# Block attention with soft mixture of experts: loads without pacing, three buffers for values, and stores of 64 rows by two

## The chip, the cores and the metric

The kernel runs on one core of a Trainium2 chip. The metric is device time in microseconds (us) of one execution; before the change it is 456.55 us, the median of three runs (453.82 to 457.1). Inputs and the output lie in the chip's memory, and every transfer between it and the core's on-chip memory is a DMA, issued here by SyncE (SP in the profile) and carried out by 16 DMA engines that belong to the core.

## What is computed

Attention inside chunks of 64 tokens (8 batches, 8 heads, 576 tokens, head size 64), then a mixture of experts in which 32 slots (8 experts with 4 each) are softmax mixtures of all 4608 tokens, and each token takes back a softmax mixture of the slots' outputs. All arrays are float32.

```python
scores = scale * np.matmul(q_c, k_c.transpose(0, 1, 2, 4, 3))      # in each chunk of 64
attn = np.exp(scores - np.max(scores, axis=-1, keepdims=True))
attn = attn / (np.sum(attn, axis=-1, keepdims=True) + 1e-09)
x = np.matmul(attn, v_c)                  # then reshaped to 4608 tokens x 512
logits = x @ phi                          # 4608 x 32
d = softmax of logits over the tokens; slot_input = d.T @ x
h = np.maximum(slot_input[e] @ w1[e], 0.0); slot_out[e] = h @ w2[e]
c = softmax of logits over the slots; out = c @ slot_out
```

q, k and v are 9.44 MB each, w1 and w2 together 33.6 MB, the output is 9.44 MB (4608 rows of 2 KB).

## The kernel before

**Units.** The attention runs over 18 units. A unit is four heads of one batch with 512 of its 576 tokens; the eight chunks of 64 tokens that are left (one of each batch) are gathered into a ninth "batch" that stands in the middle of the list. `load_qk(n)` loads a unit's keys and queries, 512 KB each, into one of two buffers (`kn`, `qn`); `load_v(n)` its values, four DMAs of 128 KB, into one of two buffers `vb`. For the ninth batch the same amounts come in more and smaller DMAs: eight of 128 KB, and eight of 64 KB with 64 partitions each.

**Turns.** `turn(n, order)` writes out one turn by hand; each engine's program is fixed in this order. In turn n TensorE (PE) makes the scores of unit n (`psc`), transposes the probabilities of unit n-1 (`pt`), transposes keys and queries of unit n+2 (`pk`, `pq`), multiplies probabilities and values of unit n-1 (`pav`) and transposes the outputs of unit n-2 (`px`). Every second turn adds the logits of a finished batch (`pl`, `pe`) or its share of the slot inputs (`pp`). VectorE (DVE) takes maxima, subtracts, normalises and copies; ScalarE (ACT) does the exponentials and the other copies. Beside each turn stand DMA issues: the keys and queries of unit n+3 ahead of it, about one of 14 weight tiles `wa` of 1 MB each (two DMAs), and the values of unit n+1 behind it.

**Pacing.** All loads of this stretch go through `dma` (line 87). It keeps a list of the loads issued and makes each new one wait until so many of the earlier ones have landed that no more than MEGA = 2^18 elements (1 MiB) are in flight. Besides, the framework gives each DMA one of eight semaphores in turn, and each engine issues its own instructions in order, so a DMA that waits holds all DMAs behind it.

**Experts.** When attention is through, its buffers become 7 more weight tiles (`wb`). The slot inputs `siT` (line 424) feed the `up` matmuls (line 544); each `up` frees four tiles, into which later weights are loaded without pacing; the `down` matmuls (line 579) accumulate all experts, `spread` copies the result, and `combine(b)` makes 512 output rows: four matmuls, four copies into a free weight tile (lines 613 and 615), four stores. In the store buffer, partition p = 64 sq + x and column block j = 2 i + kh hold row x of chunk 4 i + 2 sq + kh. Before the change, store j takes all 128 partitions of one column block, and they go to chunks c and c + 2:

```python
            c = 4 * (j // 2) + j % 2
            nc.sync.dma_start(rows[c:c + 3:2], ov[:, j])
```

Of the kernel before, what the change touches and what calls it, by code (L numbers as in the profile page):

```python
# [8 lines left out]
F32 = mybir.dt.float32  # L9
# [6 lines left out]
def kernel(  # L16
# [10 lines left out]
    nc = tc.nc  # L27
# [3 lines left out]
    B, H, S, D = q.shape  # L31
    P = 128
    CH = 64
    H2 = P // 2
    NC = S // CH
    UC = 8
    HG = H // 2
# [5 lines left out]
    REST = B  # L43
    vs = list(range(B // 2)) + [REST] + list(range(B // 2, B))
    NL = len(vs)
    NU = 2 * NL
    E, _, FF = w1.shape
    SL = phi.shape[1]
# [2 lines left out]
    EPS = 1e-9  # L51
    NWA = 14
    NWB = 7
    NV = 2
    NQK = 2
    MEGA = 2 ** 18

    HALF = (slice(0, H2), slice(H2, P))
    QUARTERS = ((0, 0), (1, 1), (0, 1), (1, 0))
# [6 lines left out]
    phi_sb = const.tile([P, NF, SL], F32, name="phi_sb")  # L66
# [10 lines left out]
    wa = [wpa.tile([P, 2048], F32, name=f"wa{i}") for i in range(NWA)]  # L77
# [3 lines left out]
    wt = {}  # L81
    worder = [(m, e, h) for m in (1, 2) for e in range(E) for h in range(2)]


    paced = []

    def dma(dst, src, pace=True):
        d = nc.sync.dma_start(dst, src).ins  # L88
        if pace:
            size = 1  # L90
            for m in dst.shape:
                size *= m
            for o in paced:
                o[1] += size
            over = [o[0] for o in paced if o[1] > MEGA]
            if over:
                tc.add_manual_dep(
                    d, over[-1].name,
                    mybir.DependencyInfo(mybir.DependencyClass.Sync, mybir.DependencyReason.DATA),
                    reason="pace")  # L100
            paced.append([d, size])

    def load_w(n, t, pace=True):
        m, e, h = worder[n]
        src = (w1[e].rearrange("(p j) f -> p (j f)", p=P)[:, 2 * FF * h:2 * FF * (h + 1)] if m == 1 else
               w2[e, DM * h:DM * (h + 1)].rearrange("(p g) f -> p (g f)", p=P))
        for i in range(2):
            dma(t[:, 1024 * i:1024 * (i + 1)], src[:, 1024 * i:1024 * (i + 1)], pace)
        t = t.rearrange("p (j f) -> p j f", j=2) if m == 1 else t.rearrange("p (g f) -> p g f", g=4)
        wt[m, e, h] = t  # L110

    with ExitStack() as actx:
        aq = actx.enter_context(tc.tile_pool(name="attn_q", bufs=1))
        a1 = actx.enter_context(tc.tile_pool(name="attn1", bufs=1))
        a2 = actx.enter_context(tc.tile_pool(name="attn2", bufs=2))
# [11 lines left out]
        at = a1.tile([P, 2, 2, HG, CH], F32, name="at")  # L127
        vb = [a1.tile([P, HG, 2, 2, D + 1], F32, name=f"vb{i}") for i in range(NV)]
        xT = [a1.tile([P, 2, 4, P], F32, name=f"xT{i}") for i in range(2)]
# [11 lines left out]
        def unit(n):  # L141
            return vs[n // 2], HG * (n % 2)

        def chunk(b, c):
            return (c, UC * CH) if b == REST else (b, CH * c)

        def load_qk(n, heads=None):
            b, h0 = unit(n)
            for src, dst in ((k, kn[n % NQK]), (q, qn[n % NQK])):
                for hs in heads or [slice(0, HG)]:  # L150
                    if b == REST:
                        for h in range(hs.start, hs.stop):
                            dma(
                                dst[:, h].rearrange("p j d -> p (j d)"),
                                src[:, h0 + h, UC * CH:S].rearrange("b (p j) d -> b p (j d)", j=4),
                            )
                    else:
                        dma(
                            dst[:, hs].rearrange("p h j d -> p h (j d)"),
                            src[b, h0 + hs.start:h0 + hs.stop, 0:UC * CH].rearrange(  # L160
                                "h (p j) d -> p h (j d)", j=4),
                        )

        def load_v(n):

            b, h0 = unit(n)
            for i in range(2):
                for sq in range(2):
                    for kh in range(2 if b == REST else 1):
                        bb, s0 = chunk(b, 4 * i + 2 * sq + kh)  # L170
                        rs, ns = (HALF[kh], CH) if b == REST else (slice(0, P), P)
                        dma(vb[n % NV][rs, :, i, sq, 0:D],
                            v[bb, h0:h0 + HG, s0:s0 + ns].rearrange("h x d -> x h d"))

        psum = {}

# [79 lines left out]
        def values(n, i):  # L256
            psum["v", i] = pp = pair(f"pav_{n}_{i}")
            for h in range(HG):
                for kh, sq in QUARTERS:
                    rs = HALF[kh]  # L260
                    nc.tensor.matmul(  # L261
                        pp[HALF[sq], kh, (D + 1) * h:(D + 1) * (h + 1)],
                        lhsT=at[rs, sq, i, h, :], rhs=vb[n % NV][rs, h, i, sq, :],
                        start=True, stop=True,
# [83 lines left out]
                    nc.tensor.transpose(out=pe[:, r, o:o + H2], in_=src[rs, :], identity=ident[rs, rs])  # L348

        def copy_e(b):  # L350
            eN = a2.tile([P, 4, SL], F32, tag="eN", name=f"eN_{b}")
            nc.scalar.copy(eN.rearrange("p (r j) s -> p r (j s)", r=2), psum["e"][:, :, 0:H2])
            lst[b][0] = eN

# [64 lines left out]
        def slots(wsel, ws):  # L419
# [17 lines left out]
        }  # L437
        batch = {
            "lg": logits, "lT": copy_l, "rm": slot_max, "eT": weights, "pe": turn_e, "eN": copy_e,
            "ca": token_max, "su": sums, "pp": partial, "pr": add_partial, "cx": token_exp, "cc": token_norm,  # L440
        }
# [7 lines left out]
        def turn(n, names):  # L449
            for x in names:  # L450
                if x in batch:
                    b = n // 2 - 2
                    if 0 <= b < NL and n % 2 == (x in odd):
                        batch[x](b)
                elif 0 <= n - lag.get(x, 0) < NU:
                    steps[x](n - lag.get(x, 0))
# [7 lines left out]
        for t in vb:  # L464
            nc.gpsimd.memset(t[..., D:D + 1], 1.0)
        load_v(0)
        nc.vector.reduce_sum(sel, ident.rearrange("p (j s) -> p s j", s=SL), axis=AX.X)
        nc.vector.tensor_copy(rep, sel.unsqueeze(1).to_broadcast([P, 4, SL]))
        nc.vector.memset(one, 1.0)
        warm(12)  # L470
        turn(-2, ["Tk", "kb", "Tq", "q"])
        load_qk(2)
        load_v(1)
        dma(phi_sb, phi.rearrange("(f p) s -> p f s", p=P))
        nw = 0
        for n in range(NU):
            if 0 < n < NU - 3:
                load_qk(n + 3)
            while nw < min(NWA, (NWA * (n + 1) + NU - 1) // NU):
                load_w(nw, wa[nw])  # L480
                nw += 1
            if n == 0:
                turn(0, ["S", "max"])
                turn(-1, ["Tk", "kb", "Tq", "q"])
                load_qk(3)
                turn(0, order[order.index("at"):])
            else:
                turn(n, order)
                if n + 1 < NU:
                    load_v(n + 1)  # L490

        b = NL - 1
        fill = wa[0][:, 0:512]
# [29 lines left out]
    def bank(name):  # L523
        return ps2.tile([P, 512], F32, tag="ps", name=name)

    wb = [wpb.tile([P, 2048], F32, name=f"wb{i}") for i in range(NWB)]
    for t in wb:
        load_w(nw, t, False)
        nw += 1
    free = []  # L530

# [5 lines left out]
    def up(e0):  # L537

        nonlocal nw
        ph = bank(f"ph_{e0}")  # L540
        for j in range(4):
            for i in range(4):
                e, h = e0 + i // 2, i % 2
                nc.tensor.matmul(  # L544
                    ph[SL * i:SL * (i + 1), :],
                    lhsT=siT[:, j, :],
                    rhs=wt[1, e, j // 2][:, j % 2, DM * h:DM * (h + 1)],
                    start=(j == 0), stop=(j == 3),
                )
        hr = f2.tile([P, 512], F32, tag="hr", name=f"hr_{e0}")  # L550
        nc.scalar.activation(hr, ph, AF.Relu, scale=rden)
        for i in range(2 * e0, 2 * e0 + 4):
            t = (wa + wb)[i]
            if nw < len(worder):
                load_w(nw, t, False)
                nw += 1
            else:
                free.append(t)
        return hr
# [45 lines left out]
    def combine(b, ss, ob):  # L605
        ov = ob.rearrange("p (j f) -> p j f", j=4)
        cT = c_all[:, 4 * b:4 * b + 4, :].rearrange("p j s -> p (j s)")
        for j in range(4):
            rs = slice(SL * j, SL * (j + 1))
            pf = bank(f"pf_{b}_{j}")  # L610
            nc.tensor.matmul(pf, lhsT=cT[rs, :], rhs=ss[rs, :], start=True, stop=True)
            if j % 2 == 0:
                nc.scalar.copy(ov[:, j], pf)
            else:
                nc.vector.tensor_copy(ov[:, j], pf)  # L615

        for j in range(4):
            if vs[b] == REST:
                rows = out.rearrange("(s x) f -> s x f", x=S)[:, UC * CH:S]
            else:  # L620
                rows = out[S * vs[b]:S * vs[b] + UC * CH].rearrange("(s x) f -> s x f", x=CH)
            c = 4 * (j // 2) + j % 2
            nc.sync.dma_start(rows[c:c + 3:2], ov[:, j])

    hrs = {}
    for e in range(0, E, 2):
# [12 lines left out]
    for b in range(NL):  # L639
        combine(b, ss, obs[b])  # L640
# [30 lines left out]
```

## Time and profile before

| | |
|---|---|
| median of three runs | 456.55 us |
| profiled execution | 455.94 us, of which the span in the trace is 454.2 us |
| PE, DVE, ACT busy | 218.3 us (48%), 135.9 us (30%), 128.1 us (28%) |
| bytes read and written | 61.93 MB, 9.44 MB |
| first and last score matmuls of a unit | 10.10 us, 200.12 us |
| slot inputs copied | 222.90 us |
| first store issued | 265.80 us |

Times in rows are microseconds from the start of the span. "Busy" is the union of an engine's instructions. The DMA share is the mean busy share of the core's 16 DMA engines. A wait names the engine and line that waited, and what ended the wait.

### The profile page before, as it was taken

To read this page: it belongs to the slowest core of one execution; us is meant where nothing else is said; L and a number is where in the kernel's file an instruction comes from. 1 tells how busy PE (TensorE), PEld (TensorE's weight loads), DVE (VectorE), ACT (ScalarE), POOL (GpSimd) and SP (SyncE) were. 2 spreads that over 40 slices of the span, in tenths; PEclk is the share of its full clock that TensorE was granted. 3 is DMA by queue.
4 is the path that set the end of the run, shared out by engine and by line. 5 is a ranking of instruction groups with operands and counts; after the bars stand their busy time and mean duration, and the time that the engine had idled before them with its cause. 6 is when DMAs were issued, how large, how long until landed. Compare 5 with 4: busy or idle time off the path is not lost.

```text
span 454.2 us, 8764 instructions
## 1 busy us (share of the span) xinstructions
PE 218.3 (48%) x3820; PEld 156.7 (35%) x3820; DVE 135.9 (30%) x281; ACT 128.1 (28%) x210; POOL 6.5 (1%) x25
## 2 busy tenths in 40 slices
PE   6659778677778675998999982000000000000000
PEld 6658666556566564875434140000000000000000
DVE  4227547564456464697300073000000000000000
ACT  4439546553446453664211062000000000000000
POOL 0000000000000000000110000000000000000000
PEclk9669889996889898899899997555555555555555
DMA  6778776775577877879999701111111111111111
GB/s 200 202 229 237 214 229 190 198 217 178 149 219 225 223 225 195 234 234 339 354 306 410 299 19 52 51 51 51 51 51 51 51 51 51 51 51 51 52 51 45
DMA packets 71710, 71.94 MB, mean 158 GB/s; under 512 B 40440, under 2 KB 58872, under 8 KB 71672
## 3 DMA queue, kind: packets, MB, share of 16 engines
q1 hardware_dynamic: 71672, 71.38, 50.2%
q8 instruction: 30, 0.49, 0.4%
q14 instruction: 8, 0.07, 0.0%
HBM read 61.93 MB, written 9.44 MB: 157 GB/s over the span
## 4 chain that ended last, share of the span: by engine, by line
DMA 37%; PE 12%; DVE 5%; SPq 4%; issue 2%; ACT 1%; DVEq 0%; ACTq 0%
DMA wa<-in_moe_w_dram 12%; DMA qn<-in_q_dram 10%; DMA kn<-in_k_dram 8%; DMA vb<-in_v_dram 7%; SPq L88 4%; PE px L285 2%; PE pq L207 2%; PE pav L261 1%; PE ph L544 1%; PE pp L379 1%; DVE xT L293 1%; DVE xs L273 1%; PE psc L224 1%; PE pd L139 1%; DVE wa L615 1%
## 5 line engine op out<-in xcount | busy, mean ns | idle before, releaser
L193 ACT COPY kb<-pk 64x512 f32<-64x512 f32 x72 | 44.9, 623 | 8.7 <-PE pk L184 8.1
L224 PE MATMUL psc<-kb,qT 128*64 128x128 f32 x576 | 38.0, 287 | 5.2 <-ACT qT L211 2.2
L207 PE MATMUL pq<-ident,qn 64*64 64x64 f32 (+1 forms) x576 | 27.6, 261 | 19.0 <-DMA qn<-in_q_dram 18.6
L211 ACT COPY qT<-pq 128x1024 f32<-128x1024 f32 x18 | 18.2, 1013 | 65.6 <-PE pq L207 65.5
L224 PEld LDWEIGHTS psc<-kb,qT 128*64 128x64 f32 x576 | 33.1, 143 | 7.8 <-DVE xT L293 2.9
L207 PEld LDWEIGHTS pq<-ident,qn 64*64 64x64 f32 (+1 forms) x576 | 24.4, 153 | 26.5 <-issue 23.5
L293 DVE COPY xT<-px 128x1024 f32<-128x1024 f32 x16 | 19.6, 1223 | 44.2 <-PE px L285 44.2
L234 DVE TENSOR_REDUCE mx<-psc 128x16 f32<-128x1024 f32 x18 | 22.0, 1221 | 18.6 <-PE psc L224 18.5
L184 PE MATMUL pk<-ident,kn 64*128 64x64 f32 x288 | 15.0, 248 | 23.3 <-DMA kn<-in_k_dram 21.3
L261 PE MATMUL pav<-vb,at 64*64 64x65 f32 x1152 | 24.5, 237 | 1.9 <-DVE xT L293 1.9
L273 DVE TENSOR_TENSOR xs<-pav,rc 128x512 f32<-128x512 f32 x36 | 24.9, 692 | 1.2
L285 PE MATMUL px<-ident,xs 128*128 128x128 f32 x144 | 24.3, 320 | 0.9 <-DVE xs L273 0.8
L261 PEld LDWEIGHTS pav<-vb,at 64*64 64x64 f32 x1152 | 21.2, 148 | 5.2 <-DVE xT L293 2.6
L237 DVE TENSOR_TENSOR sc<-psc,mx 128x1024 f32<-128x1024 f32 x18 | 21.9, 1219 | 0.4
L184 PEld LDWEIGHTS pk<-ident,kn 64*128 64x128 f32 x288 | 12.4, 156 | 26.5 <-issue 22.8
L254 ACT COPY at<-pt 128x1024 f32<-128x1024 f32 x18 | 18.2, 1013 | 9.9 <-PE pt L251 9.9
L285 PEld LDWEIGHTS px<-ident,xs 128*128 128x128 f32 x144 | 19.1, 164 | 4.8 <-issue 2.7
L243 ACT ACTIVATE sc<-sc 128x1024 f32<-128x1024 f32 x18 | 19.0, 1055 | 2.1 <-DVE sc L237 2.1
L544 PE MATMUL ph<-wa,siT 128*32 128x512 f32 x112 | 15.7, 647 | 0.0
L579 PE MATMUL po<-wa,hz 128*32 128x512 f32 x88 | 13.2, 595 | 1.1 <-DMA wa<-in_moe_w_dram 1.0
L251 PE MATMUL pt<-ident,sc 64*128 64x64 f32 x288 | 12.8, 229 | 1.0 <-ACT sc L243 1.0
L251 PEld LDWEIGHTS pt<-ident,sc 64*128 64x128 f32 x288 | 10.4, 139 | 4.2 <-issue 3.1
(87 smaller groups left out, 195.0 us busy)
## 6 DMA issues: line engine op xcount, KB each, us to landing
wa<-in_moe_w_dram SPq DMA_DIRECT2D x50, 512.0 KB
vb<-in_v_dram SPq DMA_DIRECT2D x64, 128.0 KB
kn<-in_k_dram SPq DMA_DIRECT2D x15, 512.0 KB
qn<-in_q_dram SPq DMA_DIRECT2D x15, 512.0 KB
wb<-in_moe_w_dram SPq DMA_DIRECT2D x14, 512.0 KB
out_dram<-wb SPq DMA_DIRECT2D x24, 256.0 KB
out_dram<-wa SPq DMA_DIRECT2D x12, 256.0 KB
kn<-in_k_dram SPq DMA_DIRECT2D x8, 128.0 KB
```

The costliest lines, as they stand in the source:

```text
L184: nc.tensor.transpose(out=pt[:, i, o:o + H2], in_=src[rs, h, 2 * j:2 * j + 2, :].rearrange("p j d -> p (j d)"), identity=ident[rs, rs])
L193: nc.scalar.copy(kbs[n % 2][HALF[a]].rearrange("x i hp c a (p j u) -> x a u (i hp) c p j", j=2, u=2)[:, a, u], pv[HALF[u], a].rearrange("x ...
L207: nc.tensor.transpose(out=pt[0:D * (1 + a), i, o:o + H2], in_=src[rs, f - D * a:f + D], identity=ident[rs, rs])
L224: nc.tensor.matmul(pp[HALF[sq], i, 256 * hp:256 * (hp + 1)].rearrange("p (a k x) -> p a k x", a=2, k=2)[:, :, kh], lhsT=qT[:, i, hp, CH * ...
L234: nc.vector.reduce_max(mx, psum["s"].rearrange("p i (r x) -> p (i r) x", x=CH), axis=AX.X)
L237: nc.vector.tensor_tensor(sc.rearrange("p i h (kh x) -> p (i h kh) x", x=CH), psum["s"].rearrange("p i (r x) -> p (i r) x", x=CH), psum["m ...
L251: nc.tensor.transpose(out=pt[:, sq, o:o + CH], in_=sc[rs, i, h, :], identity=ident[rs, rs])
L261: nc.tensor.matmul(pp[HALF[sq], kh, (D + 1) * h:(D + 1) * (h + 1)], lhsT=at[rs, sq, i, h, :], rhs=vb[n % NV][rs, h, i, sq, :], start=True, ...
L273: nc.vector.tensor_tensor(xs[b % 2][:, 2 * i:2 * i + 2, HG * D * g:HG * D * (g + 1)].rearrange("p k (h d) -> p k h d", d=D), av[..., 0:D], ...
L285: nc.tensor.transpose(out=psum["x"][:, hp, P * j:P * (j + 1)], in_=xs[b % 2][:, j, f:f + P], identity=ident)
L293: nc.vector.tensor_copy(d, r)
L544: nc.tensor.matmul(ph[SL * i:SL * (i + 1), :], lhsT=siT[:, j, :], rhs=wt[1, e, j // 2][:, j % 2, DM * h:DM * (h + 1)], start=(j == 0), sto ...
```

## The change

The list that paces the loads goes; a load now waits for its buffer and for its semaphore's last DMA alone. Values get a third buffer. A unit's loads stand behind each turn in the order keys and queries (of unit n+4), weights, values (of unit n+2). The tile `eN` has one buffer in place of two. A store now takes one half of the partitions and two column blocks, which are two neighbouring chunks of 64 rows.

```diff
-    NV = 2
+    NV = 3
     NQK = 2
-    MEGA = 2 ** 18
 
...
-
-    paced = []
-
-    def dma(dst, src, pace=True):
-        d = nc.sync.dma_start(dst, src).ins
-        if pace:
-            size = 1
-            for m in dst.shape:
-                size *= m
-            for o in paced:
-                o[1] += size
-            over = [o[0] for o in paced if o[1] > MEGA]
-            if over:
-                tc.add_manual_dep(
-                    d, over[-1].name,
-                    mybir.DependencyInfo(mybir.DependencyClass.Sync, mybir.DependencyReason.DATA),
-                    reason="pace")
-            paced.append([d, size])
-
-    def load_w(n, t, pace=True):
+    def load_w(n, t):
         m, e, h = worder[n]
         src = (w1[e].rearrange("(p j) f -> p (j f)", p=P)[:, 2 * FF * h:2 * FF * (h + 1)] if m == 1 else
                w2[e, DM * h:DM * (h + 1)].rearrange("(p g) f -> p (g f)", p=P))
         for i in range(2):
-            dma(t[:, 1024 * i:1024 * (i + 1)], src[:, 1024 * i:1024 * (i + 1)], pace)
+            nc.sync.dma_start(t[:, 1024 * i:1024 * (i + 1)], src[:, 1024 * i:1024 * (i + 1)])
...
-                        dma(vb[n % NV][rs, :, i, sq, 0:D],
-                            v[bb, h0:h0 + HG, s0:s0 + ns].rearrange("h x d -> x h d"))
+                        nc.sync.dma_start(
+                            vb[n % NV][rs, :, i, sq, 0:D],
+                            v[bb, h0:h0 + HG, s0:s0 + ns].rearrange("h x d -> x h d"),
+                        )
 
...
-            eN = a2.tile([P, 4, SL], F32, tag="eN", name=f"eN_{b}")
+            eN = a2.tile([P, 4, SL], F32, tag="eN", name=f"eN_{b}", bufs=1)
...
         for n in range(NU):
-            if 0 < n < NU - 3:
-                load_qk(n + 3)
-            while nw < min(NWA, (NWA * (n + 1) + NU - 1) // NU):
-                load_w(nw, wa[nw])
-                nw += 1
             if n == 0:
                 turn(0, ["S", "max"])
                 turn(-1, ["Tk", "kb", "Tq", "q"])
                 load_qk(3)
                 turn(0, order[order.index("at"):])
+                load_qk(4)
             else:
                 turn(n, order)
-                if n + 1 < NU:
-                    load_v(n + 1)
+                if n + 4 < NU:
+                    load_qk(n + 4)
+            while nw < min(NWA, (NWA * (n + 1) + NU - 1) // NU):
+                load_w(nw, wa[nw])
+                nw += 1
+            if n + 2 < NU:
+                load_v(n + 2)
 
...
-        for j in range(4):
-            if vs[b] == REST:
-                rows = out.rearrange("(s x) f -> s x f", x=S)[:, UC * CH:S]
-            else:
-                rows = out[S * vs[b]:S * vs[b] + UC * CH].rearrange("(s x) f -> s x f", x=CH)
-            c = 4 * (j // 2) + j % 2
-            nc.sync.dma_start(rows[c:c + 3:2], ov[:, j])
+        if vs[b] == REST:
+            rows = out.rearrange("(s x) f -> s x f", x=S)[:, UC * CH:S]
+        else:
+            rows = out[S * vs[b]:S * vs[b] + UC * CH].rearrange("(s x) f -> s x f", x=CH)
+        for i in range(2):
+            for sq in range(2):
+                c = 4 * i + 2 * sq
+                nc.sync.dma_start(rows[c:c + 2].rearrange("k x f -> x k f"), ov[HALF[sq], 2 * i:2 * i + 2])
 
```

The other lines of the diff put `nc.sync.dma_start` in place of `dma`, and drop an argument.

On SP, which issues every DMA, the loads of the third and fourth turn stand as follows (kn and qn are the buffers of keys and queries, vb those of values, wa weight tiles; the numbers tell buffers apart). Before:

```order
L88 DMA wa_80<-in_moe_w_dram 128x1024 x2
L88 DMA vb_115<-in_v_dram 128x4x64 x4
L88 DMA kn_108<-in_k_dram 128x4x256
L88 DMA qn_106<-in_q_dram 128x4x256
L88 DMA wa_81<-in_moe_w_dram 128x1024 x2
L88 DMA vb_116<-in_v_dram 128x4x64 x4
L88 DMA kn_107<-in_k_dram 128x4x256
L88 DMA qn_105<-in_q_dram 128x4x256
```

After, with what each waits for (DMAHW0 to 7 are the eight DMA semaphores, PE the matmuls that read the buffer last):

```order
L138 DMA qn_106<-in_q_dram 128x4x256 [waits DMAHW4_49,PE_49]
L88 DMA wa_80<-in_moe_w_dram 128x1024 [waits DMAHW5_49]
L88 DMA wa_80<-in_moe_w_dram 128x1024 [waits DMAHW6_49]
L152 DMA vb_115<-in_v_dram 128x4x64 [waits DMAHW7_49,PE_49]
L152 DMA vb_115<-in_v_dram 128x4x64 [waits DMAHW0_49]
L152 DMA vb_115<-in_v_dram 128x4x64 [waits DMAHW1_49,PE_49]
L152 DMA vb_115<-in_v_dram 128x4x64 [waits DMAHW2_49]
L138 DMA kn_107<-in_k_dram 128x4x256 [waits DMAHW3_49,PE_49]
L138 DMA qn_105<-in_q_dram 128x4x256 [waits DMAHW4_49,PE_49]
L88 DMA wa_81<-in_moe_w_dram 128x1024 [waits DMAHW5_49]
```

The values moved behind the weights and are those of a later unit, and each load waits for the DMA eight places ahead of it in place of those that the pacing names.

At the end of SP's program stand the stores (out_dram, from the tiles that combine fills). Before:

```order
L88 DMA wa_89<-in_moe_w_dram 128x1024 x2
L623 DMA out_dram<-wa_90 2x64x512 x4
L623 DMA out_dram<-wa_91 2x64x512 x4
L623 DMA out_dram<-wa_92 2x64x512 x4
L623 DMA out_dram<-wb_3424 2x64x512 x4
L623 DMA out_dram<-wb_3425 2x64x512 x4
```

After:

```order
L88 DMA wa_89<-in_moe_w_dram 128x1024 x2
L607 DMA out_dram<-wa_90 64x2x512 x4
L607 DMA out_dram<-wa_91 64x2x512 x4
L607 DMA out_dram<-wa_92 64x2x512 x4
L607 DMA out_dram<-wb_3426 64x2x512 x4
L607 DMA out_dram<-wb_3427 64x2x512 x4
```

Their number and place are the same; the outermost size on the memory's side is 64 in place of 2.

## Rows read from the trace of the kernel before

**Rows 1.** The page: its first line, the slices of the span (40 equal ones; digits are tenths), and the bytes moved.

```profile
span 454.2 us, 8764 instructions
...
PE   6659778677778675998999982000000000000000
...
DMA  6778776775577877879999701111111111111111
GB/s 200 202 229 237 214 229 190 198 217 178 149 219 225 223 225 195 234 234 339 354 306 410 299 19 52 51 51 51 51 51 51 51 51 51 51 51 51 52 51 45
...
HBM read 61.93 MB, written 9.44 MB: 157 GB/s over the span
```

**Rows 2.** The view of stretches: from and to, length, busy time and count of PE, PE's weight loads, DVE, ACT and POOL, the granted clock of PE as a share of full speed, the DMA share, GB/s.

```profile
10.00:200.00 190.00, 142.50 (x3060) 119.33 (x3060) 101.49 (x195) 99.61 (x158) 2.40 (x6) 0.87 0.76 211
...
120.00:123.00 3.00, 3.00 (x56) 2.06 (x56) 1.98 (x3) 1.11 (x2) 0.00 (x0) 0.88 0.39 85
...
184.00:200.00 16.00, 15.18 (x396) 12.74 (x396) 13.92 (x29) 11.22 (x19) 0.40 (x1) 0.95 0.83 229
...
242.00:256.00 14.00, 13.78 (x120) 4.15 (x118) 0.29 (x2) 1.15 (x3) 0.00 (x0) 1.00 1.03 408
...
275.00:435.00 160.00, 0.00 (x0) 0.00 (x0) 1.08 (x2) 0.49 (x1) 0.00 (x0) 0.51 0.13 51
```

**Rows 3.** The timeline from 222 to 300 us, single rows of ACT, PE, SP and DVE: start, length, engine, line, operation, what it writes and reads, count, and in brackets the idle time before it. DVE's last copies into the store buffers run from 268.83 for 7.26 us, to 276.1.

```profile
222.90 0.27 ACT L424 COPY siT<-pst 128x128 f32<-128x128 f32 x1 [3.81 <-PE pst L423]
...
260.26 1.05 PE L579 MATMUL po<-wa,hz 128*32 128x512 f32 x4 [0.21 <-DMA wa<-in_moe_w_dram]
...
265.80 35.67 SPq L623 DMA_DIRECT2D out_dram<-wa  x9
...
268.83 7.26 DVE L615 COPY wb<-pf 128x512 f32<-128x512 f32 x12
```

**Rows 4.** The waits of SP's queue and of PE over the whole span: who waited for what, us in total, times, the longest.

```profile
SPq L88 <- DMA wa<-in_moe_w_dram: 39.2, 37, 2.2
SPq L88 <- DMA vb<-in_v_dram: 30.5, 15, 3.8
SPq L88 <- DMA qn<-in_q_dram: 29.6, 16, 3.1
SPq L88 <- DMA kn<-in_k_dram: 28.5, 18, 3.5
...
PE pk L184 <- DMA kn<-in_k_dram: 21.3, 14, 3.2
PE pq L207 <- DMA qn<-in_q_dram: 18.6, 15, 2.3
```

**Rows 5.** The chain of waits that ended last, a piece of it in order of time: start, length, what; a DMA's length is from issue to landing.

```profile
24.25 4.62 DMA kn<-in_k_dram
28.91 4.52 DMA kn<-in_k_dram
33.45 4.04 DMA wa<-in_moe_w_dram
...
39.07 3.61 DMA vb<-in_v_dram
42.70 4.72 DMA qn<-in_q_dram
```

**Rows 6.** The timeline of PE from 185 to 201 us, two turns and the start of a third; columns as in rows 3.

```profile
185.78 1.97 PE L224 MATMUL psc<-kb,qT 128*64 128x128 f32 x32
187.67 0.71 PE L251 MATMUL pt<-ident,sc 64*128 64x64 f32 x16
188.22 0.68 PE L184 MATMUL pk<-ident,kn 64*128 64x64 f32 x16
...
189.83 1.16 PE L207 MATMUL pq<-ident,qn 64*128 64x64 f32 x32
...
193.33 1.97 PE L224 MATMUL psc<-kb,qT 128*64 128x128 f32 x32 [0.22 <-DVE xT L293]
...
198.44 0.28 PE L348 MATMUL pe<-ident,eT 64*128 64x64 f32 x2 [0.46 <-ACT eT L328]
...
200.12 1.09 PE L224 MATMUL psc<-kb,qT 128*64 128x128 f32 x16 [0.25 <-DVE xT L293]
```

**Rows 7.** The timeline of PE from 8 to 12 us: the first unit's score matmuls.

```profile
10.10 2.20 PE L224 MATMUL psc<-kb,qT 128*64 128x128 f32 x30 [2.16 <-ACT qT L211]
```

**Rows 8.** The timeline of SP: issues of loads, with the time that issuing them took, waits among them included. The eight at 117.69 are values of the ninth batch, 64 partitions each.

```profile
28.91 0.37 SPq L88 DMA_DIRECT2D kn<-in_k_dram  x1
...
16.89 2.04 SPq L88 DMA_DIRECT2D vb<-in_v_dram  x4
...
117.69 6.14 SPq L88 DMA_DIRECT2D vb<-in_v_dram  x8
```

**Rows 9.** SP's issue of the first weights behind attention, and the view of stretches (columns as in rows 2) while those weights are loaded and the experts are computed.

```profile
204.61 12.55 SPq L88 DMA_DIRECT2D wb<-in_moe_w_dram  x14
...
205.00:217.00 12.00, 10.13 (x237) 6.94 (x226) 8.49 (x25) 5.42 (x10) 0.40 (x1) 1.00 1.00 345
220.00:240.00 20.00, 19.65 (x146) 7.90 (x149) 3.42 (x17) 2.85 (x6) 2.89 (x10) 0.91 0.90 326
240.00:260.00 20.00, 19.12 (x149) 6.03 (x141) 0.58 (x4) 2.03 (x4) 0.00 (x0) 1.00 0.92 369
```

More of the change, by code (lines that the diff above doesn't have):

```diff
@@ L152, in load_qk @@
                         for h in range(hs.start, hs.stop):
-                            dma(
+                            nc.sync.dma_start(
                                 dst[:, h].rearrange("p j d -> p (j d)"),
@@ L157, in load_qk @@
                     else:
-                        dma(
+                        nc.sync.dma_start(
                             dst[:, hs].rearrange("p h j d -> p h (j d)"),
@@ L171, in load_v @@
                         rs, ns = (HALF[kh], CH) if b == REST else (slice(0, P), P)
-                        dma(vb[n % NV][rs, :, i, sq, 0:D],
-                            v[bb, h0:h0 + HG, s0:s0 + ns].rearrange("h x d -> x h d"))
+                        nc.sync.dma_start(
+                            vb[n % NV][rs, :, i, sq, 0:D],
+                            v[bb, h0:h0 + HG, s0:s0 + ns].rearrange("h x d -> x h d"),
+                        )
         psum = {}
@@ L473 @@
         load_v(1)
-        dma(phi_sb, phi.rearrange("(f p) s -> p f s", p=P))
+        nc.sync.dma_start(phi_sb, phi.rearrange("(f p) s -> p f s", p=P))
         nw = 0
         for n in range(NU):
-            if 0 < n < NU - 3:
-                load_qk(n + 3)
-            while nw < min(NWA, (NWA * (n + 1) + NU - 1) // NU):
-                load_w(nw, wa[nw])
-                nw += 1
             if n == 0:
@@ L527 @@
     for t in wb:
-        load_w(nw, t, False)
+        load_w(nw, t)
         nw += 1
@@ L554, in up @@
             if nw < len(worder):
-                load_w(nw, t, False)
+                load_w(nw, t)
                 nw += 1
```

## The prediction

> **What bounds the kernel now.** I read the slices of the span first. The three compute engines are busy for the first 60% of it, and then for 40% nothing but DMA works, at one tenth of the DMA engines and some 51 GB/s [rows 1]. So two stretches decide, and I took them apart with the view of stretches. In the last one (275 to 435 us) the DMA share is 0.13 at 51 GB/s, with PE at 0.00 busy; in the weights' stretch (242 to 256 us) the same DMA engines give 408 GB/s at a share of 1.03 [rows 2]. 0.13 is 2 of 16 engines, and 51 is an eighth of 408: the stores run on two engines, each at full speed. The last copies into the store buffers are done at 276.1 us [rows 3], so the span's last 178 us wait for nothing but stores. The arithmetic closes: 9.44 MB written [rows 1] at 51 GB/s are 185 us, after the first store at 265.80 [rows 3] that makes 450.8 of a span of 454.2.
>
> In the first stretch (10 to 200 us) PE is busy 142.5 of 190 us, DVE 101.5, ACT 99.6, and the DMA share is 0.76 at 211 GB/s [rows 2]: no resource is full. The waits say why. SP, which issues every load, waits 127.8 us in total for earlier loads to land (39.2 + 30.5 + 29.6 + 28.5) [rows 4]; these are mostly the pacing waits. PE waits 39.9 us for keys and queries (21.3 + 18.6) [rows 4]. The chain of waits from 20 to 47 us is loads one behind another, each 3.6 to 4.7 us from issue to landing [rows 5]: 1 MiB in flight over some 4.5 us of latency is 233 GB/s, close to the 211 measured.
>
> **The change part by part.**
>
> *Loads in the attention stretch.* Without the pacing list a load waits for its buffer (a PE semaphore) and for the DMA eight places ahead in SP's program, as the order with waits shows; eight loads are one unit's keys, queries, weights and values, 2.5 MiB in place of 1. So the queue should stay filled, and the next limit is PE's turn. One turn that had its loads in time ran from 185.78 to 193.33, 7.55 us, with PE without a gap; the next, from 193.33 to 200.12, took 6.79 without the two transposes of k and q (0.68 and 1.16) and with 0.22 and 0.46 us of waits on DVE and ACT [rows 6], so 8.6 at most with them. Mean: 8.1 us, over 17 turns 137.7 us, in place of the 190.0 from the first score matmul at 10.10 [rows 7] to the last turn's at 200.12. **Gain 52.3 us.** Two bounds: taking PE's 39.9 us of waits out of 190.0 and nothing else leaves 150.1 (gain 39.9); 17 turns of 7.55 leave 128.4 (gain 61.7). I take the middle value, because granted clock in the stretch was 0.87 and was 0.95 where PE ran almost without gaps [rows 2], so waits that go also make the work shorter. DMA could limit as well: a share of 0.76 over 190 us is 144 us of full work, 6.7 more than I take, but at the 408 GB/s of the weights' stretch the same 40.1 MB need only 98 us, so part of the 0.76 is packets that start on an idle queue.
>
> *The new order of a unit's loads* (weights ahead of values, values two units ahead in a third buffer) costs nothing by itself: v of unit n+2 is issued at the end of turn n and first read in turn n+3, two turns (16 us) later, against the 3.6 us of a v load [rows 5]. k and q of unit n+4 are issued when turn n has transposed unit n+2, and needed two turns later. What SP pays is the issue: 0.37 us for a large load, some 2.0 us for four of v [rows 8], in all about 3.5 us of a turn of 8; for the two units of leftover rows 8 small loads take 6.14 us with their waits [rows 8], still inside a turn. If the cover goes there, one or two turns grow by 2 to 4 us; that is inside the bounds above. The third buffer's memset is one 0.1 us instruction at the start. One eN buffer in place of two makes ACT's eN copy wait for the partial sums of the batch before, a turn and more earlier: nothing. The third buffer moves the addresses under the weight tiles that are loaded at the end of attention; their waits still name attention's last readers. I bound this by 3 us either way.
>
> *From attention's end to the first store.* The slot inputs are copied at 222.90, PE is busy for 19.65 and 19.12 us of the next two 20 us, and the last down matmul starts at 260.26, 0.21 us after its weights land [rows 3, 9]. Loads and matmuls both fill this stretch, none of it changes, so it moves as a block: 200.12 to 265.80 stays 65.7 us. First store at 265.8 - 52.3 = **213.5 us**.
>
> *Stores.* Now 64 partitions stand outermost on both sides, in place of 2 rows blocks. Loads of that form are in the trace, the leftover values (64x4x64): in 120 to 123 us, when eight of them are in flight [rows 8], the DMA share is 0.39 [rows 2], three times 2/16, so such a shape is not held to two engines. On all 16 at the 25.5 GB/s that each of two gives now, 408 GB/s, 9.44 MB take **23.1 us**. No row shows sixteen engines reading 64 partitions at once; if every pair of engines gets the speed of one, 204 GB/s, it is **46.3 us**. The nearest row, those loads, moves 85 GB/s at share 0.39, so 218 at a full share, where the whole first stretch has 278 (211 at 0.76): no halving, though engines so lightly used prove little. I take the middle, 34.7 us, and keep both ends. [...] SP's issue, at 0.5 us a store as for v (2.04 for four [rows 8]), is 36 x 0.5 = 18 us, under the transfers, and the copies end 10.3 us after the first store [rows 3]; both lie beside. The last store lands some 3.3 us after the transfers before it, as now (450.8 to 454.2).
>
> **Sum.** 213.5 + 34.7 + 3.3 = 251.5 us of span. The profiled execution took 455.94 at a span of 454.2, so 1.7 more: **253 us**. It stands 0.6 under the median of 456.55, which I leave out.
>
> **The rivals.**
> - [...] Chance 0.25.
> - *Stores at full rate, turns at PE's best*: 23.1, with 52.3 to 61.7 gained: 242 to 232 us. Chance 0.17.
> - *The loads gain nothing* (the change doesn't do what it says: the wait on the eighth DMA ahead paces as before, or keys and queries now land behind weights): the first store stays at 265.8, and 305 us come out with 34.7 for the stores. For it: landing times grow as more is in flight. Against: the 14 wb loads, issued from 204.61 us without pacing, already fill the DMA engines: a share of 1.00 and 345 GB/s from 205 to 217 us [rows 9]. Chance 0.07.
> - *Slower than before: stores on one engine.* Place: each store's split over engines; price: 9.44 MB at 25.5 GB/s, 370 us, so 213.5 + 370 + 3.3 + 1.7 = 589 us. It decides from where the stores get less than 40 GB/s (9.44 MB in the 238 us between 213.5 and the old end), 1.6 engines. Against it is the 0.39 of the 64-row loads. Chance 0.01.
> - *My forecast*: 0.48, with its own range of 241 (23.1) to 266 (gain 39.9). What is left, 0.02, is a fault I have not seen.
>
> **How the numbers follow.** The range reaches from full-rate stores with turns between 7.55 and 8.1 (about 235) to half-rate stores with the smaller gain (265 + 12.4 = 277), and a little over: 234 to 280. Under it lies some part of the second rival (0.05), above it the third and fourth and some of the rest (0.12). A measurement tells 1% (4.6 us) from no change; every case but the fourth is far faster: 0.98 faster, 0.005 within 1%, 0.015 slower.
>
> **What would show it.** In the changed profile: SP's waits for loads far under 128 us; PE's waits on kn and qn below 10 us, with score matmuls 7.5 to 8.5 us apart; the first out_dram store between 204 and 226 us; then a stretch of stores at a share near 1 with 200 to 400 GB/s, 23 to 46 us long. [...] The prediction is wrong if turns stay near 11 us with SP still waiting for DMAs, if the stretch from the last scores to the first store grows past 66 us because attention no longer covers the first weights, or if the stores' share stays under 0.3.

## The result and the profile after

The changed kernel takes **268.66 us** (median of four, 265.93 to 272.23), beside 455.19 us for the kernel before in the same comparison: a ratio of 0.588 (95% interval 0.582 to 0.595). Forecast were 253 us in a range of 234 to 280. The profiled execution's span is 266.4 us. Here and below some runs of a kernel took longer than its others; a ratio is formed without them, so it need not be the ratio of the medians.

The page's first line and slices of the changed kernel, to set beside [rows 1]:

```profile
span 266.4 us, 8773 instructions
...
PE   7687969986898596998788998888999996960000
...
DMA  6899999977699699999999999994599990588887
GB/s 209 237 245 370 255 283 349 283 208 178 192 271 322 186 230 242 342 282 270 308 338 261 256 274 328 393 352 180 164 359 415 407 383 12 157 271 251 264 261 216
```

The tail with the DMA engines at one tenth is gone: six slices of stores at 5 to 8 tenths remain.

The view of stretches of the changed kernel (columns as in [rows 2]): from the first unit's scores to the last one's, and inside the stores.

```profile
10.00:162.50 152.50, 128.28 (x3060) 107.37 (x3060) 101.90 (x195) 100.65 (x159) 2.40 (x6) 0.97 0.96 270
...
235.00:260.00 25.00, 2.17 (x14) 0.74 (x12) 3.38 (x6) 2.74 (x5) 0.00 (x0) 0.58 0.87 262
```

Against the first row of [rows 2], the same 3060 matmul records now lie in 152.5 us in place of 190, at a DMA share of 0.96 in place of 0.76. Share times length is 146.4 us here and 144.4 before: the DMA engines did the same work with the idle time taken out. The stores run at 262 GB/s and a share of 0.87, in place of 51 and 0.13.

The marks of time, from the timelines of PE, ACT and SP:

```profile
11.18 2.19 PE L206 MATMUL psc<-kb,qT 128*64 128x128 f32 x18 [2.65 <-ACT qT L193]
...
162.56 1.97 PE L206 MATMUL psc<-kb,qT 128*64 128x128 f32 x32 [0.25 <-DVE xT L275]
...
185.98 0.27 ACT L406 COPY siT<-pst 128x128 f32<-128x128 f32 x1 [3.81 <-PE pst L405]
...
227.63 11.07 SPq L607 DMA_DIRECT2D out_dram<-wa  x12
```

The seventeen turns take 151.4 us (190.0 before); from the last scores to the first store it is 65.1 us (65.7 before); from the first store to the end 38.8 us (188.4 before). So of the 187.8 us by which the span fell, 149.6 come from the stores and 38.2 from what stands before the first store: 38.6 from the turns and 0.6 from the block behind them, less the 1.1 by which the first scores came later (11.18 in place of 10.10).

PE's waits, to set beside [rows 4]:

```profile
PE pav L243 <- issue: 4.0, 5, 1.0
PE pq L189 <- DMA qn<-in_q_dram: 3.9, 3, 2.1
PE psc L206 <- issue: 3.6, 3, 1.7
PE pq L189 <- issue: 3.0, 3, 2.1
...
PE pk L166 <- DMA kn<-in_k_dram: 1.8, 1, 1.8
...
PE pp L361 <- issue: 1.5, 1, 1.5
```

The waits for keys and queries fell from 39.9 to 5.7 us. But four lines are of another kind: 12.1 us in which PE waited for nothing that the view shows ("issue"), against 0.6 before.

### The profile page after: what moved, and what is told of

It is laid out like the page before. It is cut to its first block, busy times and chain, and to the rows that moved or that the text cites. A ratio compares the mean times of both kernels' runs of the same rounds, so it can differ in the third digit from the quotient of the medians.

```text
span 266.4 us, 8773 instructions
## 1 busy us (share of the span) xinstructions
PE 204.7 (77%) x3820; PEld 146.7 (55%) x3820; DVE 136.5 (51%) x281; ACT 128.0 (48%) x210; POOL 6.5 (2%) x26
## 4 chain that ended last, share of the span: by engine, by line
PE 46%; DMA 19%; DVE 10%; issue 6%; ACT 6%; SPq 2%; DVEq 0%; POOL 0%; ACTq 0%; POOLq 0%
DMA wa<-in_moe_w_dram 14%; PE psc L206 11%; PE px L267 6%; PE pq L189 6%; DVE xT L275 6%; DMA qn<-in_q_dram 4%; PE pd L119 4%; PE pp L361 3%; PE pt L233 3%; PE pk L166 3%; PE pf L594 3%; ACT kb L175 3%; PE pav L243 2%; PE pl L283 2%; DMA out_dram<-wa 1%
## 5 line engine op out<-in xcount | busy, mean ns | idle before, releaser
L206 PEld LDWEIGHTS psc<-kb,qT 128*64 128x64 f32 x576 | 32.7, 141 | 12.1 <-issue 4.2
L189 PE MATMUL pq<-ident,qn 64*64 64x64 f32 (+1 forms) x576 | 22.5, 229 | 7.9 <-DMA qn<-in_q_dram 3.9
L243 PE MATMUL pav<-vb,at 64*64 64x65 f32 x1152 | 23.3, 222 | 5.5 <-issue 4.0
L189 PEld LDWEIGHTS pq<-ident,qn 64*64 64x64 f32 (+1 forms) x576 | 19.5, 128 | 13.9 <-issue 7.3
L243 PEld LDWEIGHTS pav<-vb,at 64*64 64x64 f32 x1152 | 19.6, 134 | 9.1 <-issue 5.7
L267 PE MATMUL px<-ident,xs 128*128 128x128 f32 x144 | 21.5, 295 | 0.6 <-DVE xs L255 0.5
L267 PEld LDWEIGHTS px<-ident,xs 128*128 128x128 f32 x144 | 16.9, 150 | 4.0 <-issue 2.2
L166 PE MATMUL pk<-ident,kn 64*128 64x64 f32 x288 | 12.7, 228 | 2.7 <-DMA kn<-in_k_dram 1.8
L527 PE MATMUL ph<-wa,siT 128*32 128x512 f32 x112 | 14.3, 594 | 0.0
L166 PEld LDWEIGHTS pk<-ident,kn 64*128 64x128 f32 x288 | 10.5, 140 | 4.5 <-ACT at L236 1.9
L233 PE MATMUL pt<-ident,sc 64*128 64x64 f32 x288 | 12.8, 229 | 0.2 <-ACT sc L225 0.2
L594 PE MATMUL pf<-ss,c_all 32*128 32x512 f32 x72 | 12.1, 727 | 0.7 <-ACT ss L585 0.7
```

The lines of the kernel that those rows point to most:

```text
L166: nc.tensor.transpose(out=pt[:, i, o:o + H2], in_=src[rs, h, 2 * j:2 * j + 2, :].rearrange("p j d -> p (j d)"), identity=ident[rs, rs])
L189: nc.tensor.transpose(out=pt[0:D * (1 + a), i, o:o + H2], in_=src[rs, f - D * a:f + D], identity=ident[rs, rs])
L206: nc.tensor.matmul(pp[HALF[sq], i, 256 * hp:256 * (hp + 1)].rearrange("p (a k x) -> p a k x", a=2, k=2)[:, :, kh], lhsT=qT[:, i, hp, CH * ...
L233: nc.tensor.transpose(out=pt[:, sq, o:o + CH], in_=sc[rs, i, h, :], identity=ident[rs, rs])
L243: nc.tensor.matmul(pp[HALF[sq], kh, (D + 1) * h:(D + 1) * (h + 1)], lhsT=at[rs, sq, i, h, :], rhs=vb[n % NV][rs, h, i, sq, :], start=True, ...
L267: nc.tensor.transpose(out=psum["x"][:, hp, P * j:P * (j + 1)], in_=xs[b % 2][:, j, f:f + P], identity=ident)
```

## The experiments

"Turns" is the time from the first unit's scores to the last one's in the profile. Medians are given with the ratio to the kernel before, measured on the same chip.

**Each half alone.** First the kernel before with the new stores, then the changed kernel with the old ones, which is the same edit the other way round (shown without the loops around the stores):

```diff
...
-            nc.sync.dma_start(rows[c:c + 3:2], ov[:, j])
...
+                nc.sync.dma_start(rows[c:c + 2].rearrange("k x f -> x k f"), ov[HALF[sq], 2 * i:2 * i + 2])
```

> The kernel before with the new stores alone. If the two halves of the change add up, the last turn's scores stay near 200 us, the first store near 266, and the stores take the 39 us they take in the changed kernel: 305 us. If the stores are that fast only because something ahead of them changed (unpaced loads, another place of the tiles), the stretch of stores is over 45 us and the time over 312.

Measured: 308.57 us, ratio 0.675 (0.670 to 0.680), between the 305 and the 312 of the two cases. Turns 194.7 us, first store 269.2, its stores again at 262 GB/s and 38.4 us from the first to the end; the 3.6 us over 305 are the longer turns and not the stores.

> The changed kernel with the stores of before. Additive: first store near 228 us as in the changed kernel, then 188 us of stores: 416 to 419 us. Rival, that part of the old stores' time came from the loads ahead: under 405 us.

Measured: 420.79 us, ratio 0.921 (0.910 to 0.932), a little over what was expected and far from the rival. Turns 152.9 us, first store 232.7, and 188.4 us from it to the end. The parts gain 148 and 36 us alone, 185 together, and 187 were measured for both (455.19 - 268.66): they lie in separate stretches and add. The new stores do what they do whatever stands ahead.

**What limits the stores.** Two edits of the changed kernel. The first reads partitions 0 to 63 in every store; the second stores 128 partitions by one column block into 128 neighbouring rows, in eight of nine batches:

```diff
-                nc.sync.dma_start(rows[c:c + 2].rearrange("k x f -> x k f"), ov[HALF[sq], 2 * i:2 * i + 2])
+                nc.sync.dma_start(rows[c:c + 2].rearrange("k x f -> x k f"), ov[HALF[0], 2 * i:2 * i + 2])
```

> The changed kernel with every store reading partitions 0 to 63, so the upper half's rows are not written right. [...] Rival, the writes or the eight DMAs in flight limit: no change, within 1.5 us.

Measured: 282.32 us, ratio 0.618 (0.613 to 0.622): 13.7 us more than the changed kernel, against no change in the rival; 11.9 of them are in the stores.

```diff
...
+            for j in range(4):
+                nc.sync.dma_start(rows[2 * j:2 * j + 2].rearrange("k x f -> (k x) f"), ov[:, j])
...
```

> The changed kernel with stores of 128 partitions by one column block into 128 neighbouring rows for eight of the nine batches, so rows come out in another order. If 64 partitions limit the stores, these run at over 350 GB/s and the stretch of stores falls from 39 us to 27 to 31, the time by 8 to 12 us. Rival, the writes limit: no change, within 1.5 us.

Measured: 257.57 us, ratio 0.564 (0.556 to 0.572). The view of stretches inside the stores, of the one-half kernel and then of the 128-partition kernel:

```profile
235.00:270.00 35.00, 4.50 (x30) 1.88 (x26) 5.71 (x10) 5.01 (x9) 0.00 (x0) 0.63 1.00 201
```

```profile
230.00:250.00 20.00, 7.69 (x53) 3.69 (x48) 8.90 (x15) 8.16 (x15) 0.00 (x0) 0.81 1.01 355
```

One half of the partitions gives 201 GB/s with all engines busy all the time (a share of 1.00), alternating halves 262, 128 partitions 355. The stretch from first store to end is 50.7, 38.8 and 28.7 us. The first edit changes which partitions the stores read and nothing else, and the rate falls from 262 to 201 GB/s: in these runs the partitions read set the rate, not the writes and not the number in flight. The 201 is close to half of the 408 of the weight loads [rows 2], 204; one such half is called a partition group below. The changed kernel, whose stores alternate between the halves, lies between. The single packets in the traces say how: a packet of 2 KB took 84 ns in the stores of the kernel before, and 162 ns on average with all stores on one half, 99% of them over 125 ns. In the changed kernel 24% of the packets were that slow, in the 128-partition kernel 6%.

The 128-partition kernel settles one thing more. Its loads are those of the run with the old stores, and in eight batches it reads the same 128 partitions of one column block; only the rows in memory differ: 128 neighbouring rows, which makes the outermost size 128, in place of two chunks that lie apart, which makes it 2. That alone takes the stores from 51 GB/s at a share of 0.13 to 355 at 1.01, and the stretch from 188.4 us to 28.7.

**The stores of one half from another queue.**

```diff
-                nc.sync.dma_start(rows[c:c + 2].rearrange("k x f -> x k f"), ov[HALF[sq], 2 * i:2 * i + 2])
+                (nc.sync, nc.scalar)[sq].dma_start(rows[c:c + 2].rearrange("k x f -> x k f"), ov[HALF[sq], 2 * i:2 * i + 2])
```

> The changed kernel with the stores of the upper 64 partitions issued by ACT, so each half has its own queue. Theory of partition groups: both queues are served in turn, so both halves are read at once; the stores reach 300 to 360 GB/s, the stretch from the first store to the end falls from 39 us to 28 to 33, the time by 6 to 11 us. Rival, packets of the two queues still meet at one half, or ACT's copies wait behind its own issues: 262 GB/s or less, no gain or a few us slower.

Measured: 260.65 us, ratio 0.568 (0.564 to 0.573).

```profile
232.00:252.00 20.00, 13.47 (x40) 6.01 (x40) 6.57 (x11) 6.89 (x13) 0.00 (x0) 0.50 1.02 337
```

The same 64-partition stores now run at 337 GB/s and end 31.8 us after the first. Both halves are indeed read at once: over this stretch both queues have packets in progress 99.9% of the time, about eight each. The gain has two parts: the engines are no longer idle at times (a share of 1.02 in place of 0.87), and fewer packets are slow (13% in place of 24%). The rival's cost is there too: ACT's copies now stretch over the stores, each pair behind two issues that together take 2 to 3 us:

```profile
226.44 1.92 ACTq L607 DMA_DIRECT2D out_dram<-wa  x2
228.46 1.07 ACT L596 COPY wa<-pf 128x512 f32<-128x512 f32 x2 [1.76 <-DVE wa L598]
229.08 2.20 ACTq L607 DMA_DIRECT2D out_dram<-wa  x2
```

but it is hidden, since the DMA share is at 1.02.

**Pacing alone.** The changed kernel with the list put back, at 1 MiB and at 2 MiB:

```diff
...
+            over = [o[0] for o in paced if o[1] > 262144]
+            if over:
+                tc.add_manual_dep(
+                    d, over[-1].name,
+                    mybir.DependencyInfo(mybir.DependencyClass.Sync, mybir.DependencyReason.DATA),
+                    reason="pace")
...
```

> The changed kernel with the pacing put back (1 MiB in flight), its order of loads, three value buffers and new stores kept. If the pacing was what held the turns, the scores of the first and the last unit are again some 190 us apart (the changed kernel: 152) and the time is 300 to 310 us; PE's waits on issue in the attention stretch fall from 12 us to under 2. Rival, the new order and the third buffer did it: under 285 us.

Measured: 307.34 us, ratio 0.672 (0.668 to 0.676); turns 190.8 us; PE waits 0.6 us on issue and 45.3 on keys and queries. At 2 MiB (524288 elements):

> The changed kernel with pacing at 2 MiB in flight. Theory that full load queues delay PE's own program (its waits on issue, 12 us in the changed kernel): these waits fall to some 6 us, while keys and queries still come in time, so the time is 262 to 268 us. Rival, that the gaps have nothing to do with the queues: the waits on issue stay at 10 us or more and the time is 268 us or above. If latency still binds at 2 MiB: over 275 us.

Measured: 267.56 us, ratio 0.585 (0.581 to 0.590); turns 150.1 us; 7.8 us on issue, which lies between the some 6 of the theory and the 10 of its rival. The view of stretches over the turns, 1 MiB and then 2 MiB:

```profile
10.00:201.00 191.00, 139.17 (x3060) 115.44 (x3060) 101.22 (x194) 99.85 (x158) 2.40 (x6) 0.88 0.74 204
```

```profile
10.50:160.60 150.10, 129.06 (x3059) 107.91 (x3060) 102.22 (x198) 99.77 (x159) 2.41 (x6) 0.97 0.96 271
```

The gain of the loads hangs on the pacing's end: with the pacing, the third buffer and the new order bring nothing that can be told (308.6 without them, 307.3 with them). Whether the pacing's end alone, in the old order, gives all of it was not run. 2 MiB in flight keep the engines as full as no pacing does (a share of 0.96 in both). Share times length is 141 and 144 us: the same work again.

**The third buffer and the leftover units.** Two value buffers, and values loaded one unit ahead, at the same place in the turn:

```diff
-    NV = 3
+    NV = 2
...
-            if n + 2 < NU:
-                load_v(n + 2)
+            if 0 < n < NU - 1:
+                load_v(n + 1)
```

> The changed kernel with two value buffers, values loaded one unit ahead at the same place. Theory that the third buffer costs and brings nothing measurable: 268 us within 2. Rival, that values then arrive late or hold keys and queries behind them: 4 us or more slower, with PE's waits on vb or on qn up.

Measured: 262.37 us, ratio 0.573 (0.568 to 0.578). Neither theory: it is *faster*, its interval clear of the changed kernel's. Turns 144.0 us. The difference lies in one place: from the scores of unit 6 to those of unit 11, where the ninth batch's small loads are issued, it takes 44.7 us, the changed kernel 51.8, and the three profiles of the first group with its loads 51.2 to 55.3. The view of stretches over the turns has the DMA engines full:

```profile
11.00:155.00 144.00, 128.03 (x3053) 106.05 (x3056) 101.89 (x195) 99.69 (x158) 2.41 (x6) 0.99 0.98 275
```

Next, the leftover units are loaded in the normal, large form, from batch 0; the line goes into both load functions:

```diff
             b, h0 = unit(n)
+            b = 0 if b == REST else b
...
```

> The changed kernel with the leftover units' keys, queries and values taken from batch 0 in the normal, larger loads, so the leftover rows come out wrong. Theory that the small loads of the two leftover units cost the shortfall of the turns around them (11.3, 9.6 and 12.8 us in place of some 8.3): those turns fall to 8 to 9 us and the time to 258 to 262 us. Rival, they are long for PE's own gaps: 266 us or more.

Measured: 262.42 us, with runs from 255.94 to 264.61 and no ratio: inconclusive as a time. In the profile, which is of the longest of the four runs, the stretch from unit 6 to 11 takes 45.7 us, the turns as a whole 147.3. The three turns that were named fell from 11.2, 9.6 and 12.8 us to 8.4, 7.6 and 9.1, but one between them grew from 10.4 to 12.1, with 1.9 us of waits on issue. So the small loads seem to cost there; what that is worth this run does not tell. Last, the third buffer kept, but values one unit ahead:

```diff
-            if n + 2 < NU:
-                load_v(n + 2)
+            if 0 < n < NU - 1:
+                load_v(n + 1)
```

> The changed kernel, three value buffers, but values loaded one unit ahead in place of two (as with two buffers). Between the scores of units 6 and 11 the profiles of the changed loads take 51 to 55 us, with two buffers 44.7. Theory that the place of the leftover values' sixteen small loads (two turns that both also load weights, ahead of later keys and queries) makes the difference: this stretch takes 44 to 47 us and the time is 262 us within 2. Rival, the third buffer itself (addresses, one wait less): the stretch stays over 50 us and the time at 268.

Measured: 263.17 us, ratio 0.572 (0.568 to 0.577); units 6 to 11 in 46.0 us. So it is not the buffer but the place: two units ahead, the sixteen small value loads stand in two turns that also load weights. PE's waits for loads from the scores of unit 6 to those of unit 11 show the difference, in the changed kernel and then in this one:

```profile
PE pq L189 <- DMA qn<-in_q_dram: 3.0, 2, 2.1
...
PE pk L166 <- DMA kn<-in_k_dram: 1.8, 1, 1.8
```

```profile
PE pav L243 <- DMA vb<-in_v_dram: 2.1, 3, 1.0
...
PE pq L189 <- DMA qn<-in_q_dram: 0.3, 1, 0.3
```

The five profiles with values two units ahead, the small loads and no pacing have 4.8 to 9.0 us of waits for keys and queries in this stretch. The three with values one unit ahead have 0 to 0.3, and 1.4 to 2.2 for values; the one with the large loads, two units ahead, has none of either. SP's timeline in the changed kernel and then in this one, with the longest issue of small values and what follows:

```profile
79.15 9.14 SPq L152 DMA_DIRECT2D vb<-in_v_dram  x8
88.39 0.55 SPq L138 DMA_DIRECT2D kn<-in_k_dram  x1
89.04 0.45 SPq L138 DMA_DIRECT2D qn<-in_q_dram  x1
89.54 2.16 SPq L88 DMA_DIRECT2D wa<-in_moe_w_dram  x2
91.80 7.63 SPq L152 DMA_DIRECT2D vb<-in_v_dram  x8
99.53 0.55 SPq L138 DMA_DIRECT2D kn<-in_k_dram  x1
100.18 0.45 SPq L138 DMA_DIRECT2D qn<-in_q_dram  x1
```

```profile
84.57 8.78 SPq L152 DMA_DIRECT2D vb<-in_v_dram  x8
93.45 0.55 SPq L138 DMA_DIRECT2D kn<-in_k_dram  x1
94.10 0.45 SPq L138 DMA_DIRECT2D qn<-in_q_dram  x1
94.61 5.98 SPq L152 DMA_DIRECT2D vb<-in_v_dram  x8
100.68 0.55 SPq L138 DMA_DIRECT2D kn<-in_k_dram  x1
```

In the first the keys and queries issued at 99.53 and 100.18 are those of unit 12, which PE needs in turn 10; it waited for the queries, and that turn took 12.8 us. The row of this wait, and the view of stretches over the turn:

```profile
105.57 1.68 PE L189 MATMUL pq<-ident,qn 64*128 64x64 f32 x32 [0.87 <-DMA qn<-in_q_dram]
...
98.52:111.34 12.82, 9.87 (x205) 8.25 (x205) 7.29 (x19) 6.45 (x13) 0.40 (x1) 0.87 0.94 258
```

The wait is only 0.87 us of that turn. PE also stood idle 0.77 us on issue and 0.84 us behind DVE, and then its granted clock fell from 1.00 to 0.50 of full speed for 3.4 us, from 106.01, so that its busy time is 9.87 us, where the like turns 6, 8 and 14 have 8.2 to 8.3. The other waits for loads in this stretch are 1.8 us for keys in turn 9 and 2.1 us in turn 6 for the queries of unit 8, a leftover unit.

In the second, unit 12's stand between the two groups of small loads, at 93.45, and no weights stand beside the second group.

**Together, and with a middle pacing.** Two value buffers and two store queues; then the same with 1.5 MiB (393216 elements) of pacing. The edits are those above.

> The changed kernel with two value buffers (values one unit ahead) and the upper half's stores issued by ACT. The two gains lie in different stretches, so they should add: 268.7 - 6.3 - 8.0 = 254.4, within 2 us. Rival, that one of them was chance or that they get in each other's way: 258 us or more.

Measured: 257.42 us (253.18 to 259.86), ratio 0.555 (0.550 to 0.559). This is the fastest of the versions that compute the whole, 4% under the changed kernel by the medians and 6% by the ratios. The time lies 3 us over the sum that was expected, just under the rival's 258; the profile has turns of 146.7 us and stores at 340 GB/s, so both gains are there.

> The same with pacing at 1.5 MiB in flight. Theory that PE's waits on issue follow from how much is queued: they fall from 9 us to 2 to 5, and the time from 254 to 248 to 252 us if the loads still come in time. Rival, that 1.5 MiB already paces: PE's waits on keys and queries over 15 us and the time 260 us or more.

Measured: 262.89 us, ratio 0.574 (0.570 to 0.578). PE's waits on issue are 2.5 us, but the profile without this pacing has 3.2 as well, so the theory gets no support here; and the time rose: turns 151.9 us, 13.5 us of waits for keys, queries and values (9.5 without), DMA share 0.92 (0.98 without). The rival's time came, but not its 15 us of waits on keys and queries: they are 6.6. 1.5 MiB already leaves the engines idle at times.

## Why the prediction was right, and where its sizes were off

*The bound, and that there are two separate stretches:* right. The parts add to within 3 us, and SP's waits for the loads of attention fell from 127.8 us to some 18 (12.2 + 4.9 + 0.8).

*The block between:* right. 65.7 us were forecast, 65.1 measured.

*The stores:* 34.7 us and 3.3 of landing were forecast, 38.8 measured. The 34.7 was the middle of two ends and not worked out, so that it came so close is in part luck. The lower end, 23.1 us, supposed 16 engines at 25.5 GB/s each. The upper, 46.3 us, is the rival of 265 us with the chance of 0.25; it supposed two engines at the speed of one, an estimate that no row or run shows. What the runs showed in its place is 201 GB/s when all stores read one half of the partitions and 355 when nearly all read 128, and that the alternation gives back about half of the loss (stretches of 50.7, 38.8 and 28.7 us). My nearest row, the leftover values, misled: at a share of 0.39 their packets of 256 bytes took 18 ns each, as in the whole first stretch, so they did not yet get in each other's way, and the row could not tell.

*The turns:* this is the term that was mis-sized. Taken was PE's pace, 17 turns of 8.1 us, 137.7; measured 151.4, a gain of 38.6 us in place of 52.3, just past the lower bound of 39.9. It is why the first store came at 227.6, past the 204 to 226 that I had named, and not at 213.5. The step that failed is the sentence that set the DMA's limit aside: a share of 0.76 over 190 us is 144 us of full work, and I let 408 GB/s, which here only the stretch of weight loads reaches, talk it down to 98 and put the rest down to packets that start on an idle queue, which no run shows. More than half of the rest is the size of the packets: in this stretch of the kernel before, the middle time of a 256-byte packet was 18 ns, of 1 KB 46 and of 4 KB 159, which is 14, 22 and 26 GB/s on an engine, and all packets at these times make some 123 us. The other 20 us are packets that took longer; why they did stays open. Nine profiles, with 1 to 2.5 MiB in flight and other orders, all have 140 to 147 us of it. With two value buffers the turns take 144.0 us at a share of 0.98, the shortest of all versions: the engines are then as good as full with this mix of loads. The other 7 us are the leftover units. The part on the clock held: 0.97 in place of 0.87, and 128.3 us of busy PE in place of 142.5 for the same matmuls.

*The new order and the third buffer at nothing:* right for the buffer (263.17 us with three, 262.37 with two), wrong by 5 to 6 us for values two units ahead. I counted two turns of slack for the values, and checked SP's time per turn alone. What I did not follow is who stands behind the leftover values in SP's queue: keys and queries of later units. I had put 2 to 4 us on one or two such turns, inside a bound that the DMA limit then used up.

*PE's waits on keys and queries below 10 us:* right (5.7). *Turns of 7.5 to 8.5 us:* true of six of seventeen; four are shorter or at 8.8, and the long ones (9.6 to 12.8) stand at the leftover units or where PE waits on issue.

*The rival that the loads gain nothing* is what the changed kernel gives with the pacing put back (307 us; 305 were worked out). *Stores on one engine* did not occur (a share of 0.87).

## What to carry to other kernels

Share times length of a stretch is the DMA engines' work, and it stayed at 140 to 147 us through all orders and depths of queue tried, while no version's turns got under 144.0: when pacing goes, take that product as the floor, not the bytes over the best rate of another kind of transfer (98 us here). In these stores an outermost size of 2 came with a DMA share of 0.13, two of 16 engines, where 64 and 128 had 0.87 and 1.01, and with 64 the partitions read set the rate (201 GB/s from one half, 262 from the halves in turn); both halves of the partitions should be in flight at once, from two queues if a store can only take one half (337 GB/s). When loads are put further ahead, follow what stands behind the slowest of them in the same queue.

## What the runs showed of the hardware that was not expected

Two queues, one for each half of the partitions, carry the same 64-partition stores at 337 GB/s, where one queue that alternates halves carries 262.

PE waits on "issue" appeared with the full queues: 0.6 to 0.9 us in all at 1 MiB in flight, 2.5 at 1.5 MiB, 7.8 at 2 MiB, and 3.2 to 14.4 without pacing. In the changed kernel the gaps are up to 2.1 us each, and many stand in the middle of a group of matmuls, as here:

```profile
137.71 1.41 PE L206 MATMUL psc<-kb,qT 128*64 128x128 f32 x21 [0.23 <-DVE xT L275]
140.86 0.87 PE L206 MATMUL psc<-kb,qT 128*64 128x128 f32 x11 [1.74 <-issue]
```

The page of the profile counts 30 packets of kind "instruction" on a queue of their own (0.8% of the 16 engines' time in the changed kernel, 0.4% before). The times of these packets, 16 KB each, fit the gaps closely. In all profiles together there are 80 waits on issue of 0.5 us or more in the stretch of the turns and shortly behind; after 77 of them PE goes on 1.25 to 1.71 us behind the landing of such a packet, where a moment taken at random would fall so with a chance of about 9%. That PE waits there for its own program, as the theory of the run at 2 MiB has it, is not shown: no view names what ended these waits, and no run changes the packets by themselves. What the gaps cost stays open too: the kernel with 1.5 MiB in flight has few of them and was slower, because its loads were late.
